# Putting 64-bit weights together as 32-bit values: the low words rounded to whole words in place, and the list of priorities replaced

## The chip, the cores and the metric

The kernel runs on one core of one Trainium2 chip. Its metric is the device time of one execution in microseconds. The core has TensorE (PE, matmuls into PSUM; PEld are its weight loads), VectorE (DVE), ScalarE (ACT), GpSimd (POOL) and SyncE (SP, which here issues every DMA). Each engine works through its own queue in order, and queues wait for one another through semaphores.

## The reference

A linear attention is followed by a two-layer block. There are 8 batches, 8 heads, 576 tokens and 64 columns a head. For q and k, `proj = x @ w_phi` has 128 features; the row's largest absolute value is taken off it, and the features are `exp(proj)` and `exp(-proj)` side by side. Then, per head,

```python
kv  = einsum('bhsf,bhsd->bhfd', k_p, v)
z   = sum over tokens of k_p
num = einsum('bhsf,bhfd->bhsd', q_p, kv)
den = einsum('bhsf,bhf->bhs', q_p, z)[..., None] + 1e-06
x   = num / den                      # 4608 tokens x 512
h   = x @ w_in                       # 512 -> 2048
out = relu(h) ** 2 @ w_out           # 2048 -> 512
```

The inputs of the attention are float32. `w_in` and `w_out` reach the kernel as 64-bit floating-point numbers.

## The kernel before, in words

**Attention.** Two heads form a pair, so there are 32 pairs (`NPAIR`), four to a batch. Keys and queries are projected on TensorE, DVE finds the largest absolute values and subtracts them (L602, L605, L714, L716), ACT takes the exponentials (L608, L610, L746, L748) and copies results out of PSUM (L310), and TensorE forms `kv`, `num` and `den`. The first six pairs (`early`, `EARLY = 6`) have a form of their own; the later ones go through `visit` and `late`, where POOL finds the largest absolute value over partitions (L943). The quotient of a pair is made at L808 and is scaled and split into two float16 parts for the block that follows (L827 or L834, then L830); both parts lie in a ring of tokens.

**The two-layer block.** The 4608 tokens are 18 chunks of 256. For each chunk, `moe` runs over eight slices `f` of 256 of the 2048 columns. The first matmuls (L1009) take the float16 parts of `w_in` (`win`), ACT and DVE form the square in two parts (L1018, L1020, L1022, L306), and the second matmuls (L1039) take `w_out` in three forms: a high part (`wh`), a low part and a bf16 copy (`wl`). The sums of one chunk over all `f` stand in two banks of PSUM, so one chunk's second matmuls are finished before the next chunk's begin. The first chunk therefore needs all sixteen pieces of weights.

**The weights.** `w_in` and `w_out` are cut into 8 pieces each, of 128 partitions x 1024 64-bit numbers, 1 MB a piece. `order_w` lists the sixteen pieces and `home_of` says which raw buffer each is loaded into. Buffers are used again: the load of a piece waits for the last reader of the piece before it there (`home_read`). The last six pieces share two buffers; pieces 3o, 6i, 7i and 7o follow one another in `x0` (the digit is `f`, i is `w_in`, o is `w_out`). A raw piece is a row of 2048 32-bit words: the low word of a number, then its high word. `join_words` makes a float32 of each pair of words:

- `size` (L450 on ACT, L452 on DVE) reads the high word as a float32 and scales it by 2 to the -111 into `u`. This brings the exponent into range.
- `low` (L456, ACT only) reads the low word as an unsigned number, scales it to between 0 and 7, and writes the rounded value, as one byte, over the lowest byte of the high word in the raw buffer. It comes after `size`, which reads that high word.
- `shift` (L460, DVE) moves `u` up by 3 bits.
- `join` (L463, DVE) takes the sign and the three low bits from the high word and joins them to `u`.

After the join, `most` (L480, ACT) writes absolute values of a piece of `w_in` over its low words, for a sum over the row. Every two such pieces give a power of two (L397 on TensorE, L403 to L408 on DVE), and `value_in` writes the two float16 parts (L529 or L530, then L532). A piece of `w_out` is split by `out_high` (L499 or L501) and `out_low` (L306 on POOL, L517 or L519). Four buffers `u` hold the joined words; `u` is taken by `size` and let go after the last of these splits. When all pieces are done, the room of `u` becomes the second half of the token ring.

**What sets the order.** Each operation is added to a `Plan` with an engine, a duration in microseconds, the operations it comes after, the buffers it uses and a rank. `other=` names a second engine with its own duration; the planner counts it as ready `LATER = 2.0` us later there. `lock=` is an allowance for the port that DVE and POOL share. `Plan.order` plays the durations through and, on each engine, takes the ready operation of the lowest rank. The instructions are issued in the resulting order, which is then fixed. The ranks of the operations whose given rank lies between -50 and 70 are replaced by those of a written-out list, `RANKS`, two characters a rank (`improve`). It holds 1107 of them, and covers the loads, the preparation of weights, the early pairs and the first part of what follows.

Of the kernel before, what the change touches and what calls it, by code (L numbers as in the profile page):

```python
# [292 lines left out]
def tile_kernel(ctx, tc, qp, kp, vp, w_phi, w_in, w_out, out):  # L293
    nc = tc.nc
    V, A, G, PE, SP = nc.vector, nc.scalar, nc.gpsimd, nc.tensor, nc.sync
    P = Plan()
# [129 lines left out]
    def fetch(n, f, of_in, rank):  # L426
        home = home_of[f, of_in]
        box = []
        src = w_in if of_in else w_out

        def load():
            box.append(cp.tile([128, 2048], I32, name=f"raw{f}{'io'[not of_in]}", tag=home))
            SP.dma_start(box[0], src[f])

        ld = P.add("SP", 0.47, load, [home_read[home]] if home in home_read else [], [], rank - 3.0 + 0.3 * n,
                   land=2.4, xfer=2.8)
        return ld, lambda: box[0][:, 0:2048:2], lambda: box[0][:, 1:2048:2], lambda: box[0].bitcast(U8)[:, 4:8192:8]

    def join_words(n, f, of_in, rank):

        home = home_of[f, of_in]
        key = [("u", n)]
        u = lambda: u_[0][n]
        ld, low_w, high_w, low_byte = fetch(n, f, of_in, rank)
        if of_in:
            spare[f] = low_w

        def size(E):
            if E is A:
                A.activation(out=u().bitcast(F32), in_=high_w().bitcast(F32), func=AF.Copy, scale=2.0 ** -111)  # L450
            else:
                V.tensor_scalar(out=u().bitcast(F32), in0=high_w().bitcast(F32), scalar1=2.0 ** -111, scalar2=None,  # L452
                                op0=ALU.mult)

        def low():
            A.activation(out=low_byte(), in_=low_w().bitcast(U32), func=AF.Copy,  # L456
                         scale=0.875 * 2.0 ** -29, bias=0.4995)

        def shift():
            V.tensor_scalar(out=u(), in0=u(), scalar1=3, scalar2=None, op0=ALU.logical_shift_left)  # L460

        def join():
            V.scalar_tensor_tensor(out=u(), in0=high_w(), scalar=word(0x80000007), in1=u(),  # L463
                                   op0=ALU.bitwise_and, op1=ALU.bitwise_or)
# [10 lines left out]
    def split_in(n, f, rank):  # L475
        o = join_words(n, f, True, rank)
        g, i = divmod(f, 2)

        def most():
            A.activation(out=spare[f]().bitcast(F32), in_=u_[0][n].bitcast(F32), func=AF.Abs, accum_out=wmax[g][:, i:i + 1])  # L480
# [652 lines left out]

DIGITS = "".join(chr(c) for c in range(33, 127) if chr(c) not in "\"\\'")[:90]
RANKS = (
    "B:HwDM8vA=A1EP2,D=EUc|UtLOUUS]TDUGLDQ8SJO=WTC3SmIyS[AhD=5!@-;CD.-THKHCQuCp?+^4IVH8MbT>X@[w[@c9[>FlEk"
    "`DCtgj^|BLM`D3`NMFGGAd@LLHR{ZDW<mq`Uv`XB`ma3QkZhJ4NaPVOCX@cuQ,Z5lBq;vUnT`wU;M>:UD/I^XIH[QAXLejY?dEOF"
    "ElP?W5NiXdS&CFBHB%A5/;,82rH70e557b4I7!-|%u-^-Z6A/x&:0$&>.f6];>3R2+;aC/2>IwE$ERUJH0F9B8P*RnVlbpFA.s2G"
    "1?1s0=;Q)J,/0J:hH#@T?i0b>a=Z:r1U4#4g4,3S0c-],k.42$11:?QWA@/V*?8J/a4;460p3*$<$;.F,a(()4#J&!$V({.1/W5U"
    "57:{Gi6Z4f>W>IBKPV<!9:G&ByAk]^GdDlA7Py[f[HLxIBFEEJA{<};^>_;gJ&2*0]&=*c.L-g<t71AqR(GfUyO<?9HwAM>wLo14"  # L1140
    ";/79=32@,&/r#=-},O+IAv.T3;#G8Y)A,2,X*x)2+%@(,K=&.d-K1%,^@@8}%94v5i:d<n<fE&Bl&k1k<&<h@k+W/12F1$85&#:Y"
    "=W@[8Z:;;F%H9V,7+8.1:s0.)xCO(Y.M+%+$.uAGDwL)>=FL>W?uEVERCp7nNb;pKw]+ZxSwS-QpcDVR[.FdQ.Q]SjXVI3G5ZoXC"
    "I,TzWzE,ZDS>JmG[BM@WE46AMPLVPAZ?JN=_GJ@5aYMU<OZ!PdXjQZI/9A9+D]Nd5?7bVr:<UkLF?!<pAL;jM=BoF8DO,+C9<[<d"
    "O{3|`+>$Zhd]]cRailV3QGW>_ZG5]BNHRROpBkKmFlUCHsY:M^]5SVDA:PA|7$1y;7Cg:TO[By7^3D*9?+CeK:SoS?J.LHScc)i*"
    "O[L@XsPIKiA.SX2UKhD%N}[%K_X*:wIGO3PC@oY[GkIk_U1k2w0D/5/O+q2Z1KCa=wC]@u=}Cs9}>4;69xE&?;=LR7MO>#H!TTUF"
    "T^VxeRM[VFTaP=XF6p?3Nv<6P#K9D4OTJjJbHPY.PkK;AmTDF-Tp[[MbN3<.MFFaX)0I8gJf?h:#H`FjJ;FZF;F;9aEME@A=HeOx"
    "Cd1[&8&g)-&6%N-20G,P-a7iFoGVRpYLY!D=P#W^A(P2Io?.Ou=JLNEFVEk9MjT*RsfzxjW/o2oPc)^2E;KkRbOjE=U<QN3Z;c:L"
    "A`YRI(UdT[HxZ!IVGE=WF=PCFm0gIw81BkGdSgHHRtEUAs>n]P_<ZRTCU#3ZFZMc]}K5GrR2FXZ2e`WBcPp_^5X7Y4MTL5N2UfF2"
    "T^FIGuO2IzQu:K;DIDA|K!Ch(l5K*`92MRCp:{IP@KKVPmUp<sOBKfN|PeI|6/KGAA0+B;PQR9=HG#GNN)V;WX>LLPK2Fa9|LqJx"
    "@CMsE:_WJFPYJUZFJX_0WyELDGN&Y^F4N]G.;#L0A_LNET4D=04PDo0)1ePn4u@tXp5lFdBEQiRuKIB,5[]%R$KhOdYr_.cE`)VK"  # L1150
    "ZYSkeUF_7vB^QG2gG;O|HUPPBi<F32B|DtIoQ>Z&_wXEd@W]MzZk[l]7a&FINNVXR#d-Oc^.I^XuQ`j9YnDGOiQ/UbF+JzAe@XN!"
    "YE4d;M?jH>DlQ<=R=KDB?}>mT>G7=AN.eBN$N$WdNm@DH{Mt>O@fY`OMGxR5UmH^R`2X7q<8?LOiM|6nBJAkGbM`J;LeHrD%_9H%"
    "PqF}V@k^ajgRxXjViI_^W_Xo_Pc?[eOoZeSvUyU/_me|d;c)J|Fm;P;hQ;Hr8vKyAXG(H0A_:37/MW9m9Y0}-7/.*!>O)>0k+,(u"
    "&M$G5%+u@G?1En+0>[K)N0?,:dNu<IRAMi=Y=V0qA&MqG;P9`nKUK(O#GdG>4&B}GtX{6JU*^?Z]NPN<NKB.GfJW8f[*T+V<]?G7"
    "40KrD$E$DD_^ZMR:NIO%MG]^cOYFMxPZSe_T].LB]R_yT^]3f?Y*Pm`EUDEpI&=I1o73)sAM8E;FO=IHAQAkFL9QKR2H-&.n)d=x"
    "AR2b?NNW9yC9N3XjeBhJ|<g&hdeP[Fc]]]P6c#U(J2AGJFCdByN/I}bKMRKcFJ=m?SJRDI@!MdRtXuQ7Ih>q`XILK@_,jVT|ITYL"
    "lNZsRH;I/qB=G<L0U*G`HlVoHp]2KZNP]}`S]IPgTMYHS+SFS/No?^I@Dr;*PG]hQ}e1TtMnTOWqZLgWYX`S^=W{[-^5G9XvT-[/"
    "D[U9Q@[wBl;qE5"
)


# [31 lines left out]
```

## Time and profile before

| | |
|---|---|
| time, median of 3 runs | 1078.0 us (1075.48 to 1078.98) |
| time of the profiled execution | 1078.0 us |
| its span, first to last instruction | 1076.2 us |
| instructions | 19519 |
| mean granted TensorE clock | 0.986 |
| L456, the rounding pass, ACT, 16 times | 2479 to 2606 ns each |
| L460, the shift, DVE, 16 times | 633 to 694 ns each |
| L463, the join, DVE, 16 times | 1210 to 1226 ns each |
| L450 / L452, the size pass | 12 on ACT, 4 on DVE |

A table of busy time by stage gives, for each stretch of the span in microseconds, the time that each engine was busy and how many instructions that was, then the granted clock of TensorE, the share of the DMA engines and the data rate. A row of the order of time gives the start and the duration in microseconds, the engine, the line of the program, what is written from what, the shapes, how many instructions the row merges, and in brackets how long the engine stood idle before it and for whom. Rows of one engine overlap a little at their ends, because a duration runs until the last write has landed.

### The profile page before, as it was taken

How to read it: one execution, taken by the hardware profiler on the slowest of the kernel's cores; microseconds unless marked ns; L12 is line 12 of the kernel's file. 1: busy time of each engine (PE TensorE's matmuls, PEld its weight loads, DVE VectorE, ACT ScalarE, POOL GpSimd, SP SyncE). 2: the span in 40 equal slices, each digit the busy share in tenths (PEclk: the TensorE clock that was granted, in tenths of full speed). 3: DMA queues.
4: the chain of work that ended last, by engine and by line, in shares of the span. 5: the costliest groups of instructions: out<-in, count | busy, mean ns of one | idle time of the engine just before them, and what ended most of it. 6: DMA issues, size and time to landing. Idle time of an engine off the chain costs nothing.

```text
span 1076.2 us, 19519 instructions
## 1 busy us (share of the span) xinstructions
PE 1038.8 (97%) x7762; PEld 711.0 (66%) x7762; DVE 730.6 (68%) x1546; ACT 655.2 (61%) x1133; POOL 137.0 (13%) x66
## 2 busy tenths in 40 slices
PE   6787899999999999999999999999999999999998
PEld 5554566666766666676666667666666666677775
DVE  5588788788877688888878777767786775111111
ACT  6799987756764557656666656665555665333333
POOL 0011113111120131101111111111011111000000
PEclk9897899999999999999999999999999999999999
DMA  9532350231122222121212111212110101000000
GB/s 362 210 115 89 114 169 32 56 104 56 48 56 65 66 65 67 56 76 56 73 48 76 50 60 44 65 56 75 39 58 28 48 10 42 12 21 20 1 21 20
DMA packets 66143, 73.47 MB, mean 68 GB/s; under 512 B 35204, under 2 KB 44036, under 8 KB 64004
## 3 DMA queue, kind: packets, MB, share of 16 engines
q1 hardware_dynamic: 66052, 72.22, 21.2%
q8 instruction: 61, 1.00, 0.4%
q14 instruction: 30, 0.25, 0.1%
HBM read 59.18 MB, written 12.99 MB: 67 GB/s over the span
## 4 chain that ended last, share of the span: by engine, by line
PE 88%; ACT 8%; DMA 2%; DVE 1%; issue 1%; SPq 0%; ACTq 0%
PE po L1039 35%; PE ph L1009 35%; PE pv L642 4%; PE pn L860 3%; PE pp L586 2%; PE pv L860 2%; PE pp L930 2%; PE pn L930 1%; PE pv L647 1%; ACT u L450 1%; PE pn L592 1%; DMA den<-sx 1%; DMA raw7i<-in_w_in_dram 1%; DMA v<-in_vp_dram 1%; ACT sx L549 0%
## 5 line engine op out<-in xcount | busy, mean ns | idle before, releaser
L1009 PE MATMUL ph<-ring,win 128*128 128x256 f16 x3456 | 402.7, 274 | 0.0
L1009 PEld LDWEIGHTS <-win 128*128 128x128 f16 x3456 | 338.0, 98 | 71.4 <-issue 8.5
L1018 ACT ACTIVATE r<-ph,cw 128x512 f32<-128x512 f32 x144 | 98.9, 687 | 235.4 <-PE ph L1009 234.9
L306 DVE TENSOR_TENSOR gl<-ph,gh 128x512 bf16<-128x512 f32 x144 | 98.5, 684 | 176.3 <-ACT ph L1022 172.5
L943 POOL PARTITION_ALL_REDUCE mx<-pt x52 | 115.9, 2229 | 616.5 <-ACT pt L310 453.6
L1039 PE MATMUL po<-wh,gh 128*128 128x512 f32 x576 | 171.5, 419 | 0.0
L1039 PE MATMUL po<-wl,gh 128*128 128x512 bf16 x576 | 149.6, 382 | 0.0
L1039 PE MATMUL po<-wl,gl 128*128 128x512 bf16 x576 | 148.0, 379 | 0.0
L1039 PEld LDWEIGHTS po<-wh,gh 128*128 128x128 f32 x576 | 98.4, 189 | 28.5 <-issue 9.1
L1039 PEld LDWEIGHTS <-gl 128*128 128x128 bf16 x576 | 56.3, 98 | 68.0
L1020 ACT ACTIVATE gh<-r 128x512 fp32r<-128x512 f32 x144 | 90.6, 629 | 4.4
L1039 PEld LDWEIGHTS <-gh 128*128 128x128 bf16 x576 | 44.8, 98 | 73.3 <-issue 39.7
L1022 ACT ACTIVATE ph<-r 128x512 f32<-128x512 f32 x144 | 84.1, 584 | 0.2
L642 PE MATMUL pv<-e,v 128*64 128x256 f32 x512 | 61.0, 380 | 0.0
L310 ACT ACTIVATE n<-pn 128x320 f32<-128x320 f32 (+1 forms) x32 | 13.8, 430 | 75.1 <-PE pn L860 74.6
L957 DVE SCALAR_TENSOR_TENSOR pt<-qe,zc,pt 128x576 f32<-128x576 f32 x52 | 42.2, 814 | 20.7 <-ACT pt L955 20.2
L306 DVE TENSOR_TENSOR qe<-pt,mx 128x576 f32<-128x576 f32 x52 | 39.1, 753 | 23.1 <-POOL mx L943 22.9
L948 ACT ACTIVATE qe<-qe 128x576 f32<-128x576 f32 x52 | 35.1, 674 | 27.9 <-DVE qe L306 27.9
L608 ACT ACTIVATE e<-e 128x512 f32<-128x512 f32 x64 | 39.7, 620 | 13.9 <-DVE e L605 13.7
L642 PEld LDWEIGHTS pv<-e,v 128*64 128x64 f32 x512 | 35.5, 137 | 15.4 <-issue 1.3
L955 ACT ACTIVATE pt<-qe,zc 128x576 f32<-128x576 f32 x52 | 40.2, 773 | 5.6 <-DVE zc L921 1.3
L894 DVE STREAM_TRANSPOSE kvs<-pv 128x256 f32<-128x256 f32 x26 | 11.6, 447 | 45.7 <-PE pv L860 44.1
(188 smaller groups left out, 1316.6 us busy)
## 6 DMA issues: line engine op xcount, KB each, us to landing
v<-in_vp_dram SPq DMA_DIRECT2D x32, 320.0 KB
k<-in_kp_dram SPq DMA_DIRECT2D x32, 288.0 KB
q<-in_qp_dram SPq DMA_DIRECT2D x32, 288.0 KB
rb<-rd SPq DMA_DIRECT2D x64, 144.0 KB
out_dram<-o SPq DMA_DIRECT2D x34, 256.0 KB
td<-kvs SPq DMA_DIRECT2D x26, 128.0 KB
kz<-td SPq DMA_DIRECT2D x104, 32.0 KB
raw0i<-in_w_in_dram SPq DMA_DIRECT2D x1, 1024.0 KB
```

The source lines that it names most:

```text
L306: eng.tensor_tensor(out=out_, in0=a, in1=b_, op=ALU.subtract)
L608: o = P.add("ACT", act_us(512), lambda n=n: A.activation(out=e_[n][:, :, 1, :], in_=e_[n][:, :, 0, :], func=AF.Exp, scale=-1.0), [o], [("e ...
L642: PE.matmul(out=to[64 * h:64 * h + 64, 0:256], lhsT=v_[p][:, t, h, :], rhs=e_[2 * p + h][:, t].rearrange("p s f -> p (s f)"), start=t == 0 ...
L860: PE.matmul(out=to[64 * h:64 * h + 64, :], lhsT=kz_[n][:, 128 * s_ + 64 * h:128 * s_ + 64 * h + 64], rhs=qe_[2 * n + h].rearrange("p (s x) ...
L943: o = P.add("POOL", par_us(S), lambda n=n, h=h: G.partition_all_reduce(mx_[n], pt_[p][:, h, :], channels=128, reduce_op=bass_isa.ReduceOp. ...
L955: o = P.add("ACT", act_us(S, 1), lambda h=h, qe=qe, y=y: A.activation(out=y(), in_=qe(0), func=AF.Copy, scale=zc_[p][:, 2 * h:2 * h + 1]), ...
L957: o = P.add("DVE", dve_us(S), lambda h=h, qe=qe, y=y: V.scalar_tensor_tensor(out=y(), in0=qe(1), scalar=zc_[p][:, 2 * h + 1:2 * h + 2], in ...
L1009: PE.matmul(out=ph[:, j, :], lhsT=win[w][:, t, 128 * ff:128 * ff + 128], rhs=ring[half][x][:, t, c0:c0 + T], start=k == 0, stop=k == 3 * K ...
L1018: o = P.add("ACT", act_us(512, 1), lambda: A.activation(out=r_[n], in_=ph_[bank], func=AF.Relu, scale=cw[:, f, 0:1]), [g1], [("ph", bank), ...
L1020: sq = P.add("ACT", act_us(512), lambda: A.activation(out=gh_[n], in_=r_[n], func=AF.Square), [o], [("r", n), ("gh", n)], Q)
L1022: o = P.add("ACT", 0.59, lambda: A.activation(out=ph_[bank], in_=r_[n], func=AF.Square), [o], [("ph", bank), ("r", n)], Q, other=("DVE", 0 ...
L1039: PE.matmul(out=po_[po[i][1]], lhsT=g[:, j, 128 * i:128 * i + 128], rhs=w[:, j, :], start=(ff == 0 and s == 0), stop=(ff == 2 * NFP - 1 an ...
```

## The change

The byte is no longer written. `low` writes its rounded value as a whole 32-bit word over the low word itself, so it waits only for the load, and it may run on ACT (planned at 1.15 us, as before) or on DVE (0.68). A pass of its own, `ends`, joins the sign of the high word to that low word, in place. The shift of `u` and the last join become one pass, which reads `u` and the low word. A piece still has four passes. All ranks in the list are replaced.

```diff
-        return ld, lambda: box[0][:, 0:2048:2], lambda: box[0][:, 1:2048:2], lambda: box[0].bitcast(U8)[:, 4:8192:8]
+        return ld, lambda: box[0][:, 0:2048:2], lambda: box[0][:, 1:2048:2]
...
-        def low():
-            A.activation(out=low_byte(), in_=low_w().bitcast(U32), func=AF.Copy,
-                         scale=0.875 * 2.0 ** -29, bias=0.4995)
-
-        def shift():
-            V.tensor_scalar(out=u(), in0=u(), scalar1=3, scalar2=None, op0=ALU.logical_shift_left)
+        def low(E):
+            to, of, a, b = low_w(), low_w().bitcast(U32), 0.875 * 2.0 ** -29, 0.4995
+            if E is A:
+                A.activation(out=to, in_=of, func=AF.Copy, scale=a, bias=b)
+            else:
+                E.tensor_scalar(out=to, in0=of, scalar1=a, scalar2=b, op0=ALU.mult, op1=ALU.add)
+
+        def ends():
+            V.scalar_tensor_tensor(out=low_w(), in0=high_w(), scalar=word(0x80000000), in1=low_w(),
+                                   op0=ALU.bitwise_and, op1=ALU.bitwise_or)
 
         def join():
-            V.scalar_tensor_tensor(out=u(), in0=high_w(), scalar=word(0x80000007), in1=u(),
-                                   op0=ALU.bitwise_and, op1=ALU.bitwise_or)
+            V.scalar_tensor_tensor(out=u(), in0=u(), scalar=3, in1=low_w(),
+                                   op0=ALU.logical_shift_left, op1=ALU.bitwise_or)
 
         sz = P.add("ACT", 1.15, lambda: size(A), [ld], key, rank, other=("DVE", 0.64, lambda: size(V), 4.0))
-        l = P.add("ACT", 1.15, low, [sz], [], rank)
-        o = P.add("DVE", 0.64, shift, [sz], key, rank, lock=4.0)
-        o = home_read[home] = P.add("DVE", 1.22, join, [o, l], key, rank, lock=4.0)
+        l = P.add("ACT", 1.15, lambda: low(A), [ld], [], rank, other=("DVE", 0.68, lambda: low(V), 4.0))
+        o = P.add("DVE", 1.22, ends, [l], [], rank, lock=4.0)
+        o = home_read[home] = P.add("DVE", 1.22, join, [sz, o], key, rank, lock=4.0)
         return o
...
 RANKS = (
-    "B:HwDM8vA=A1EP2,D=EUc|UtLOUUS]TDUGLDQ8SJO=WTC3SmIyS[AhD=5!@-;CD.-THKHCQuCp?+^4IVH8MbT>X@[w[@c9[>FlEk"
...
+    ">-88CNJ8R[-H?$EnS^A/FORAPUPUF1bR</BBDdK?[)T-Gvk=9djyUJ@&Ngk0WUW`QfRJc%^3[{itSEiwp/l$];JC[t>|K{-6H`,C"
...
```

More of the change, by code (lines that the diff above doesn't have):

```diff
@@ L19 @@
 U32 = mybir.dt.uint32
-U8 = mybir.dt.uint8
 AF = mybir.ActivationFunctionType
@@ L443, in join_words @@
         u = lambda: u_[0][n]
-        ld, low_w, high_w, low_byte = fetch(n, f, of_in, rank)
+        ld, low_w, high_w = fetch(n, f, of_in, rank)
         if of_in:
@@ L1135 @@
 RANKS = (
-    "B:HwDM8vA=A1EP2,D=EUc|UtLOUUS]TDUGLDQ8SJO=WTC3SmIyS[AhD=5!@-;CD.-THKHCQuCp?+^4IVH8MbT>X@[w[@c9[>FlEk"
[L1137 to L1155, printed above, removed]
@@ L1156 @@
-    "AR2b?NNW9yC9N3XjeBhJ|<g&hdeP[Fc]]]P6c#U(J2AGJFCdByN/I}bKMRKcFJ=m?SJRDI@!MdRtXuQ7Ih>q`XILK@_,jVT|ITYL"
-    "lNZsRH;I/qB=G<L0U*G`HlVoHp]2KZNP]}`S]IPgTMYHS+SFS/No?^I@Dr;*PG]hQ}e1TtMnTOWqZLgWYX`S^=W{[-^5G9XvT-[/"
-    "D[U9Q@[wBl;qE5"
+    ">-88CNJ8R[-H?$EnS^A/FORAPUPUF1bR</BBDdK?[)T-Gvk=9djyUJ@&Ngk0WUW`QfRJc%^3[{itSEiwp/l$];JC[t>|K{-6H`,C"
+    "M`J^CT]MX^?wC3[jU/J5Of9NYuFY:IOY6d)vMhT@O^FGU:d0D{S`9ySAV<rGLDJiKu5.<V;Wa*dsXtd)a$E(6wH7NT[g^:WPvDt2"
+    "lHsXs:xErHigT%Dbely3;2ejjox6rTo8]biYfvIlBvB^-XG*;L/)/|>48S77<]:H4K2:@s@aFALX@F>[IXTNRDItAd:r7e4P0c=J"
@@ new lines @@
+    ";XJi4bG$kei7M-H|6)a>BSLH2mBSEu:c7WGB?H@RO(*Z5m/+691I#Q6R.f%H5}>g3g&U#t.@Lb&l:`Gf9L/u4?(F/()|(o&k*m;P"
+    "0p+,;K4rOK*S.E0t6-4-$1(Y$A$w0q?$9W0^KH,-?}P?BM-{=O=q);AQ$=$D#f$E$0(<15(](9)b%,*&)Q%n,9$W+<#Q#-&7&y-%"
+    "#K3O<|&|,u1&1P80*x5gB@;h,t5L,_/v(K4}&#$R4E.x)k4A#w;P*C57#i11-A-T)tM9%HTcJ^:NKQ/IVhP_C,SFPN2q6>NFSe0r"
+    "I=<3,M5z;eK!)7($(m#=9j=(?Z2c(6;oBm:n/+6C-%8ZD29dDX@H^uW0;!,gA@QW@`B@.e4eF24{-8.y1v?wGu2E7e(e2AOL;+Vl"
+    ":UKq7bQ^@Z4^LY_U&9Fu,YgYAJ>&1qH|onK_XFL1ZoG>@-ehKZTc_T>leQ?)B1L[9{=DQu6dOCNE8<.UAe:sI2>*?+O@`fZSvvRL"
@@ new lines @@
+    "e3fwEUVZ6^Oh2T)N#J-X(x@llyNJS;N`dYB)DgdmK(R^G+Ai9.AUL-8m6w&VK$($1:<I&d,H5Y*..-D@A<ALSwCQ964bQZQ^J!G1"
+    "/T1LBX.?Cp=z58/V+,5BA/.xSSC=7)0qKrIFZk8L6,DPMwBEY[-p(c;3kcFpfhO|0WC{I`ehY}d3KG^n7Ge#QYUWL#cnV>IW5d=4"
+    "r{C[YP]Ia&ZOZII6Fw?q@C0.Jag8:a>^;-BOD!GRGTG%DMp+W@TMF(9,QPL1PTC+)J5X.8(m)`)[)*(=6v9mP3A?H9O9:/ECT>$H"
+    ",RN]?/)+/c%i)q+/Gx^(6i9A1RdbK5V<2g@ebtH$Aa<k5;UW^4iyk/lfi0j|u?udNgsMbeu0oqk{vAzxw[^E[<fIYh^Ue=U8T0LT"
+    ">p6JB(;h5^9{A*M/KMTaa<i>:VN%617L3+)6#D#D-UD-#DP,=?*-&X1+OKX|]cQhhAgkQBl]TOnuHft@Y:HqhGLu6A6C8uKvG$kP"
@@ new lines @@
+    "KHI[[/<G9N]XnjiY2[[LHS=KAras{CTlu?|_hSdygw|a|`ljiUo=WHP8j#YZHNbwfaJps1c+m{r,aQ^MiUJyHLPQ^?o)dSZ;R&RS"
+    "Op8}DbH9,/24,hPfNJe9?oRX5o5;CMQ9Q!Dr7[>(/{?y608+6`TiEce=|Wq=RhP)PT?aU{O/T*Q17fA-.D$3#729#99B?<ZjAF<M"
+    "H!=ZcpSXQ8?@]{Q3S;TNWq96;kCFHAG,^hXXl4]l^UZ9KrcgGcB;M9KhQ+K:TaZOpDbL_tGId@j)bso,o(kYa%dHuBr|dDW.W^b5"
+    "ww_qs+1Z:<WHMay]6g=o_x=.?nO-FcYmyD{/|,aQa#Uv|?|mcRL2FVgb4;534c2eW`@tU@/x5]5@)*<U6TPiCQ_.AHF&+K3JB7UV"
+    "P)T8/lX0<J9a;31;;694/H:j2)?:?BT!E|Lw<BRSI*H_W+@u4T5U<$:)BcN{F(;PE#Fw7kQ:MR[Hv&IzCS=#MkWRdug6V?yf{}tM"
@@ L1159 @@
+    "N4hprUuwbT]Ilpa>v5Nh;7IOJRo$npb:RholbCgoSrBURX:G.)I!=O/g;mS;)2%uZlM<auq;VTRfXPVi_YH0QieC?*F1T2B47%9G"
+    "Z/D}RPa?poIuCR>dQX2=.J3H4G&i)G/-(2/4(J2wF;3^8;9^KUU|DgE&3u3BF2=HAo.bcpbdB`M?ZACD[5.CHC`XKcaETPiVV.P&"
+    "C$HgMu?v=k[#e.K*H^_j[+e,Vl](OBae]Ug>[,UtiF^,|tx>s#TEn}bUI[pdgQj/f4PnN;::B<o!P}QFY`NjVNFWYZcwCwSFf]bx"
+    "h#B.S&BcI]OvWo8g@{Z1Zjf#rFxU](c#AIH*JW7??#4Hc?.Q9&)}XgL.[iNImeGY@U0)LMK:cf5^x(X[cOP[i_`mUi>D*sDOA*K#"
+    "WHbaOV`eTME>J."
 )
```

## The prediction

> **What bounds the kernel now.** I read the busy times and the slices of the page first, then a table of busy time by stage, then the order of time on each engine inside the stage that has the slack. All figures are of the one profiled execution, 1078.0 us long, of which the span is 1076.2 and 1.8 lie outside it; the median of the runs shown is 1078.0 too, so no correction stands between them.
>
> ```profile
> span 1076.2 us, 19519 instructions
> PE 1038.8 (97%) x7762; PEld 711.0 (66%) x7762; DVE 730.6 (68%) x1546; ACT 655.2 (61%) x1133; POOL 137.0 (13%) x66
> PE   6787899999999999999999999999999999999998
> DVE  5588788788877688888878777767786775111111
> ACT  6799987756764557656666656665555665333333
> ```
>
> ```profile
> core 0: us, PE busy (x) PEld busy (x) DVE busy (x) ACT busy (x) POOL busy (x), PEclk, DMA share, GB/s
> 0.00:40.00 40.00, 26.06 (x281) 19.02 (x281) 20.13 (x46) 26.16 (x46) 0.68 (x6) 1.00 0.94 365
> 40.00:170.00 130.00, 110.19 (x966) 73.42 (x967) 103.21 (x168) 120.36 (x170) 19.87 (x8) 0.88 0.34 109
> 170.00:1076.00 906.00, 902.50 (x6517) 618.56 (x6515) 607.27 (x1333) 508.64 (x920) 116.44 (x53) 1.00 0.17 49
> 118.70:170.00 51.30, 47.95 (x348) 32.55 (x347) 41.61 (x67) 46.43 (x62) 10.57 (x5) 0.94 0.36 122
> ```
>
> From 170 us on TensorE is busy 902.50 of 906.00 us: nothing there can be won or hidden, and whatever makes TensorE full earlier comes off the end one for one. Up to 40 us the DMA share is 0.94 and ACT is busy only 26.16 of 40: that stage waits for loads. Between 40 and 170 us TensorE idles 130 - 110.19 = 19.8 us, and its clock is 0.88 there, so up to 0.12 x 110.19 = 13.2 us more are lost to slow matmuls. In that stage ACT is the fullest engine, 120.36 of 130 us (0.926); DVE has 103.21 (0.79). After 118.70 TensorE idles only 51.30 - 47.95 = 3.4 us, so most of the slack, 16.4 us, lies between 40 and 118.70. That is where the sixteen weight pieces are put together beside the first six head pairs, and what TensorE waits for there is ACT:
>
> ```profile
> 96.13 2.15 PE L773 MATMUL pn<-qe,kz 128*32 128x288 f32 x16 [4.03 <-ACT n L310]
> 115.79 1.11 PE L737 MATMUL pp<-ident,pt 128*128 128x128 f32 x4 [3.84 <-ACT qe L748]
> ```
>
> **The change, part by part.** *The rounding pass on ACT (L456).* Today it reads 1024 unsigned 32-bit words, each 8 bytes from the last, and writes single bytes, also 8 bytes apart. An engine's rows overlap at their ends, so I price by the distance from start to start.
>
> ```profile
> 66.23 1.14 ACT L450 ACTIVATE u<-raw1o 128x1024 f32<-128x1024 f32 x1
> 67.28 0.47 ACT L310 ACTIVATE kvs<-pv 128x384 f32<-128x384 f32 x1
> ...
> 73.46 2.50 ACT L456 ACTIVATE raw1o<-raw1o 128x1024 uint8<-128x1024 uint32 x1
> 75.70 2.61 ACT L456 ACTIVATE raw3i<-raw3i 128x1024 uint8<-128x1024 uint32 x1
> ```
>
> The byte pass holds ACT for 75.70 - 73.46 = 2.24 us. A pass over the same 1024 words that reads 4 bytes at the same spacing and writes 4-byte values (L450) holds it for 67.28 - 66.23 = 1.05 us. The changed pass reads as the first and writes 4-byte words 8 bytes apart. L480 already writes 4-byte values into that place, in 39.97 - 38.97 = 1.00 us:
>
> ```profile
> 38.97 1.10 ACT L480 ACTIVATE raw1i<-u 128x1024 f32<-128x1024 f32 x1
> 39.97 0.18 ACT L480 ACTIVATION_READ_ACCUMULATOR raw1i<-u 128x1 f32 x1
> ```
>
> No row shows whole words from unsigned words on ACT. The bounds are 1.05 (L450, the price of reading and writing 4 bytes at all) and 2.24 (L456 as it is). I take 1.05: four of the five things that the new pass does (length, spacing of the read, spacing and width of the write) are in the 1.05 rows, and only the unsigned read is not. The gain is 1.19 us a pass.
>
> ```profile
> 0.00:40.00 40.00, 5.04 (x2) 1.00 0.94 365
> 40.00:118.70 78.70, 22.23 (x9) 0.85 0.33 101
> 118.70:170.00 51.30, 12.28 (x5) 0.94 0.36 122
> ```
>
> These are L456's passes by stage: 2 in the load-bound part, where 2 x 1.19 us buy nothing; 9 between 40 and 118.70; 5 after it. ACT in the stage falls by 14 x 1.19 = 16.7, from 120.4 to 103.7 us.
>
> By the Trainium skill ("ScalarE: Activation LUTs", section "What ACT_TABLE_LOAD costs"), ACT takes one element per cycle for every function, in fp32 and bf16 alike, and an ACTIVATE with immediate scale and bias 186 ns + 0.833 ns an element: an estimate of 1.04 us for these 1024. The 2.50 us row does not obey it. By that rule the types cannot be what makes the pass slow, the change of type would buy nothing, and the time would be that of the rival on the unsigned read, below.
>
> *The sign and the join on DVE.* The shift of u (L460) goes; its work is folded into the last join. A pass that takes the sign of the high word into the low word comes in; the join stays one pass.
>
> ```profile
> 29.48 1.23 DVE L463 SCALAR_TENSOR_TENSOR u<-raw1i,u 128x1024 int32<-128x1024 int32 x1 [1.12 <-ACT raw1i L456]
> 30.62 0.28 DVE L612 TENSOR_REDUCE kmt<-pn 128x1 f32<-128x128 f32 x1
> ...
> 72.90 0.68 DVE L452 TENSOR_SCALAR u<-raw3i 128x1024 f32<-128x1024 f32 x1
> 73.61 0.69 DVE L460 TENSOR_SCALAR u<-u 128x1024 int32<-128x1024 int32 x1
> 74.22 0.28 DVE L615 TENSOR_TENSOR et<-pn,kmt 128x128 f32<-128x128 f32 x1
> ```
>
> Old: 0.61 (L460) + 1.14 (L463). New: 1.14 + 1.14. DVE pays 0.53 us a piece more: 14 x 0.53 = 7.4 in the stage, 103.2 + 7.4 = 110.6 us. The new sign pass has both inputs and its output spaced; L463 has one input spaced. Bounds: 1.14, and twice that, 2.28, were the spacing to cost a full pass; I take 1.14 because the spaced L452 runs in 0.68 like the dense L460.
>
> *The second way, on DVE.* The rounding pass may now run on DVE, which the planner prices at 0.68. The nearest row is L452 (0.68, spaced read, same length), 0.61 from start to start; the upper bound is 1.14 (L463), were its types or its spaced write to halve the rate. Each pass so moved takes 1.05 off ACT and puts 0.61 on DVE. With DVE already the fuller engine by 110.6 to 103.7, I take none moved on balance for the sum. Fully levelled, the two would have (110.6 + 103.7) / 2 = 107.2 us each.
>
> *The order inside a piece.* The byte pass had to wait for the size pass, since it overwrote a byte of the word that the size pass reads. The new pass needs the load alone. Before, the path of a piece was 1.05 + 2.24 + 1.14 = 4.4 us; now it is 1.05 + 1.14 + 1.14 = 3.3, with the size pass beside it. Behind the sign pass on DVE wait that engine's maxima and subtractions for the next head pair, which is in the 7.4 us. The last pieces share one raw buffer, so each load waits for the piece before it:
>
> ```profile
> 116.34 0.33 SPq L433 DMA_DIRECT2D raw6i<-in_w_in_dram  x1
> ...
> 136.37 0.33 SPq L433 DMA_DIRECT2D raw7i<-in_w_in_dram  x1
> ...
> 151.82 0.33 SPq L433 DMA_DIRECT2D raw7o<-in_w_out_dram  x1
> ```
>
> If only that chain counted, its three pieces give 3 x 1.1 = 3.3 us.
>
> *The list.* All 1107 ranks are replaced, so the order on every queue, SP's loads among them, changes in the stages up to 170 us. The old list was made with 1.15 us for a pass that takes 2.24; the new one prices the same pass at 1.15. For the order itself the trace bounds it by its largest stall that is due to order alone:
>
> ```profile
> 38.24 0.74 ACT L549 ACTIVATE sx<-v 128x640 bf16<-128x640 f32 x1 [5.49 <-DMA den<-sx]
> ```
>
> ACT stands 5.49 us in front of a late load. The new order may lose this (a gain of 5.5) or have one more (a loss of 5.5); I take zero.
>
> *The sum.* Way one, by the fullest engine: DVE with 110.6 us, as full as ACT is today (0.926), needs 110.6 / 0.926 = 119.4 us for what takes 130: 10.6 us less. Way two, by place: the 9 passes before 118.70 us give 9 x 1.19 = 10.7; the five after it lie beside a TensorE that has 3.4 us of idle time left, and I count nothing for them (without that cover they would be worth 5 x 1.19 = 6.0 more). Both say 10.6. Forecast: 1078.0 - 10.6 = 1067.4 us. Its own range runs from the chain alone (1078.0 - 3.3 = 1074.7) to the whole ACT relief (1078.0 - 16.7 = 1061.3).
>
> **The rivals.**
> *The unsigned read is what costs 2.24 us.* For it: no 1.05 us row reads unsigned words. Against it: the byte write is just as new to those rows. Then ACT keeps 120.4 us unless passes move. All 14 on DVE make it 110.6 + 14 x 0.61 = 119.1 us, and 119.1 / 0.926 = 128.6: 1.4 us won; none moved wins nothing. About 1077.
>
> *The raw-buffer chain sets the end.* For it: the three issues above, 15 to 20 us apart. Against it: TensorE idles only 3.4 us after 118.70. 1074.7.
>
> *The new order also loses the 5.49 us stall*, beside the full 16.7: 1078.0 - 22.2 = 1055.8. For it: 33 us of idle time and slow clock are there to be won. Against it: up to 40 us the DMA share is 0.94, and an order cannot make loads faster.
>
> *Slower: DVE becomes the bound, through the port that it shares with POOL.*
>
> ```profile
> 79.78 2.62 POOL L306 TENSOR_TENSOR wl<-u,wh 128x1024 bf16<-128x1024 f32 x1 [13.13 <-ACT wh L499]
> 120.63 2.74 POOL L306 TENSOR_TENSOR wl<-u,wh 128x1024 bf16<-128x1024 f32 x1 [1.50 <-DVE wh L501]
> ```
>
> ```profile
> 80.08 2.93 DVE L808 TENSOR_TENSOR rb<-n,rb 128x576 f32<-128x576 f32 x1
> ...
> 121.18 3.27 DVE L532 SCALAR_TENSOR_TENSOR win<-u,cw,win 128x1024 f16<-128x1024 f32 x1
> ...
> 125.56 1.28 DVE L532 SCALAR_TENSOR_TENSOR win<-u,cw,win 128x1024 f16<-128x1024 f32 x1
> ```
>
> A DVE pass that starts inside one of POOL's runs till POOL has ended: 3.27 for 1.28 us, 2.0 lost. POOL is busy 19.87 of the 130 us, 0.15. Were the planner to send all 14 rounding passes to DVE, 28 passes are new there (sign and rounding): 28 x 0.15 x 2.0 = 8.4 us on top of 119.1 make 127.5, and 127.5 / 0.926 = 137.7: 7.7 later, 1085.7. It decides once DVE carries more than the 120.4 us that ACT has now, that is, from 120.4 - 110.6 = 9.8 us of moved passes and held ports on. Against it: the planner counts 2 us against a pass on its second engine, and the removed shift was open to the same hold. By the Trainium skill ("SBUF — State Buffer", section "Who interferes with whom") a DVE instruction with two SBUF inputs, or in a two-port mode, and a POOL one that reads SBUF exclude each other for the whole instruction; the four rows agree with it.
>
> **How the numbers follow.** About 0.3%, 3.2 us, is what a measurement can tell from no change. Chances: forecast 0.55 (faster 0.93, same 0.05, slower 0.02 of it), unsigned read 0.16 (0.3, 0.5, 0.2, for the order may fall either way), buffer chain 0.09 (0.65, 0.3, 0.05), stall lost as well 0.08 (all faster), DVE bound 0.12 (0, 0.3, 0.7). Faster: 0.512 + 0.048 + 0.058 + 0.080 = 0.70. Same: 0.028 + 0.080 + 0.027 + 0.036 = 0.17. Slower: 0.011 + 0.032 + 0.004 + 0.084 = 0.13. The range reaches from 1055, just past the case where the stall is lost as well (1055.8), to 1080, past the unsigned read (1077) and into the DVE case by as much as the 3.2 us of a measurement; what it leaves out is most of the DVE case, some 0.09, and about 0.06 below.
>
> **What would show it.** The rounding pass, written as int32 from uint32, at about 1.14 us on ACT and 0.68 on DVE: right; at 2.5: the unsigned read. The sign pass at 1.2 us on DVE. Between 40 and 170 us ACT busy well under 120 and DVE over it or near; a TensorE that is full, with no idle time of 3 us or more, from about 108 instead of 118.70; the last of the weight pieces joined near 155 instead of 165. DVE over 0.93 of that stage beside idle time of TensorE that ends on DVE would show the slower case. The forecast is wrong if ACT's relief is there and TensorE's idle time before its full stage is still 16 us or more.

## The result, and the profile after

The changed kernel takes 1064.59 us (median of 4 runs, 1063.47 to 1066.1) against 1077.55 us before: a ratio of 0.9889, 95% interval 0.9876 to 0.9903. That is faster by 12.0 us (10.4 to 13.4), where 10.6 were forecast. Below, each ratio is turned into microseconds by (ratio - 1) x 1077, since the runs of the kernel before that stand beside an experiment differ by a microsecond or two from one experiment to the next.

The page of the changed kernel, its span, its busy times and three rows of the 40 slices:

```profile
span 1064.3 us, 19450 instructions
PE 1028.1 (97%) x7676; PEld 705.8 (66%) x7762; DVE 745.1 (70%) x1549; ACT 632.0 (59%) x1130; POOL 136.2 (13%) x66
PE   7788999999999999999999999999999999999998
DVE  6799987987977868889878777867686775111111
ACT  6798876656666556756666655665565565333333
```

TensorE is at 9 tenths or more from the fifth slice on, before only from the sixth (a slice is 27 us). Of its matmuls 86 have no record here (7676 against 7762 weight loads), so its busy time after 170 us isn't compared. Busy time by stage of the changed kernel (engines in the order PE, PEld, DVE, ACT, POOL, then clock, DMA share, GB/s):

```profile
0.00:40.00 40.00, 29.22 (x320) 21.42 (x320) 31.05 (x59) 28.00 (x50) 0.68 (x6) 1.00 0.95 366
40.00:170.00 130.00, 113.65 (x1008) 74.56 (x1012) 115.17 (x190) 104.43 (x177) 24.27 (x9) 0.96 0.33 109
```

Between 40 and 170 us ACT is down from 120.36 to 104.43 us, DVE up from 103.21 to 115.17. TensorE's idle time there fell only from 19.8 to 16.4 us; its clock rose from 0.88 to 0.96, so by the estimate of the prediction slow matmuls cost up to (1 - 0.96) x 113.65 = 4.5 us where they cost up to 13.2. In the load-bound 40 us before it DVE does 31.05 us of work where it did 20.13.

The passes of a piece in the changed kernel, by line: the rounding pass on ACT (L457) and on DVE (L459), the sign pass (L462).

```profile
L457 ACT ACTIVATE raw3o<-raw3o x1: 1263/1263/1263, 28.9 to 28.9; 128x1024 int32<-128x1024 uint32 x1
L457 ACT ACTIVATE raw5i<-raw5i x1: 1107/1107/1107, 34.5 to 34.5; 128x1024 int32<-128x1024 uint32 x1
...
L459 DVE TENSOR_SCALAR raw6o<-raw6o x1: 676/676/676, 138.9 to 138.9; 128x1024 int32<-128x1024 uint32 x1
...
L462 DVE SCALAR_TENSOR_TENSOR raw7o<-raw7o x1: 1234/1234/1234, 150.2 to 150.2; 128x1024 int32<-128x1024 int32 x1
```

The first two are the longest and the shortest of twelve on ACT; four are on DVE. From start to start the next work on ACT follows after 1.01 to 1.11 us, so the passes are at the prices taken. The order of time on SP, and then on ACT for piece 3i:

```profile
125.48 0.33 SPq L432 DMA_DIRECT2D raw7i<-in_w_in_dram  x1
...
139.34 0.35 SPq L432 DMA_DIRECT2D raw7o<-in_w_out_dram  x1
```

```profile
13.43 1.12 ACT L457 ACTIVATE raw3i<-raw3i 128x1024 int32<-128x1024 uint32 x1 [0.48 <-DMA raw3i<-in_w_in_dram]
...
76.93 1.17 ACT L449 ACTIVATE u<-raw3i 128x1024 f32<-128x1024 f32 x1
```

The last pieces' loads are issued 10.9 and 12.5 us earlier than before (136.37 and 151.82), about as much as the whole gain. That the loads are what sets the end is not shown by it. And piece 3i is rounded at 13.43 us, 63 us ahead of its size pass (L449): the old order could not do that, for the byte pass waited for the size pass, which needs one of four `u` buffers.

### The profile page after: what moved, and what is told of

The parts are those of the page before. It is cut to its first block, busy times and chain, and to the rows that moved or that the text cites. A ratio compares the mean times of both kernels' runs of the same rounds, so it can differ in the third digit from the quotient of the medians.

```text
span 1064.3 us, 19450 instructions
## 1 busy us (share of the span) xinstructions
PE 1028.1 (97%) x7676; PEld 705.8 (66%) x7762; DVE 745.1 (70%) x1549; ACT 632.0 (59%) x1130; POOL 136.2 (13%) x66
## 4 chain that ended last, share of the span: by engine, by line
PE 86%; DVE 6%; DMA 4%; ACT 3%; issue 1%; SPq 0%; DVEq 0%; ACTq 0%
PE po L1042 34%; PE ph L1012 33%; PE pv L645 5%; PE pn L863 3%; PE pp L589 2%; PE pv L863 2%; PE pp L933 2%; DMA den<-sx 1%; PE pn L933 1%; PE pv L650 1%; PE pn L595 1%; DVE u L466 1%; DMA rd<-rc 1%; DVE rb L811 1%; DMA rb<-rd 1%
## 5 line engine op out<-in xcount | busy, mean ns | idle before, releaser
L946 POOL PARTITION_ALL_REDUCE mx<-pt x52 | 113.4, 2180 | 619.1 <-ACT pt L309 437.7
L1042 PE MATMUL po<-wl,gh 128*128 128x512 bf16 x504 | 134.1, 381 | 4.9
L645 PE MATMUL pv<-e,v 128*64 128x256 f32 x512 | 63.4, 388 | 7.3 <-ACT kz L309 5.4
L964 DVE STREAM_TRANSPOSE yt<-pt 128x576 f32<-128x576 f32 x52 | 40.4, 776 | 1.5
```

What stands on the lines that cost most here:

```text
L645: PE.matmul(out=to[64 * h:64 * h + 64, 0:256], lhsT=v_[p][:, t, h, :], rhs=e_[2 * p + h][:, t].rearrange("p s f -> p (s f)"), start=t == 0 ...
L946: o = P.add("POOL", par_us(S), lambda n=n, h=h: G.partition_all_reduce(mx_[n], pt_[p][:, h, :], channels=128, reduce_op=bass_isa.ReduceOp. ...
L964: o = P.add("DVE", dve_us(S), lambda n=n, y=y: V.transpose(yt_["y", n - 2 * EARLY], y()), [o], [("pt", p), ("yt", ("y", n - 2 * EARLY))], ...
L1042: PE.matmul(out=po_[po[i][1]], lhsT=g[:, j, 128 * i:128 * i + 128], rhs=w[:, j, :], start=(ff == 0 and s == 0), stop=(ff == 2 * NFP - 1 an ...
```

## The experiments

**The price of the byte pass alone.** The old order, with one word changed in it:

```diff
-            A.activation(out=low_byte(), in_=low_w().bitcast(U32), func=AF.Copy,
+            A.activation(out=low_w(), in_=low_w().bitcast(U32), func=AF.Copy,
```

> The kernel before, its list and its order of instructions, with one edit: the rounding pass on ACT writes a whole 32-bit word over the low word instead of a byte into the high word. The join is as it was, so the three lowest bits of every weight keep the high word's own three lowest bits: the low word is left out of the weights. No sign pass, no new list, DVE's work unchanged. Theory (the price of the byte pass is the gain): ACT is relieved by 14 x 1.19 = 16.7 us between 40 and 170 us, and the time falls by 10 to 17 us, to 1061 to 1068. Rival (the new list, or the freer order inside a piece, is the gain): less than 4 us, 1074 or more.

Measured: 1059.88 us, ratio 0.9843 (0.9826 to 0.9859), 16.9 us faster. By stage, in that run:

```profile
40.00:170.00 130.00, 118.44 (x1059) 81.02 (x1065) 115.33 (x202) 113.77 (x189) 25.23 (x10) 0.94 0.37 114
```

The price of the pass is worth more than the whole gain of the change, and nearly all of the 16 x 1.19 = 19.0 us that ACT is spared comes off the end. The theory stands; what comes with the change besides must cost about 5 us.

The edit also does a second thing. The byte lay in the high word, which the join reads; the whole word does not, so the join no longer reads what the rounding pass writes. In the trace before, DVE waits 11.6 us for that pass in front of twelve joins (who waited for L456):

```profile
  DVE u L463: 11.6, 12
```

In this run's trace there is no such wait. Every join there starts 0.06 us or more after the rounding pass of its piece has ended, so with the shorter pass the wait would have cost next to nothing even if the join still had to have it. How much of the 16.9 us is ACT's time and how much these waits of DVE, no run separates.

**No rounding at all.** The old order again, without the pass:

```diff
-            A.activation(out=low_byte(), in_=low_w().bitcast(U32), func=AF.Copy,
-                         scale=0.875 * 2.0 ** -29, bias=0.4995)
+            pass
...
-            V.scalar_tensor_tensor(out=u(), in0=high_w(), scalar=word(0x80000007), in1=u(),
+            V.scalar_tensor_tensor(out=u(), in0=high_w(), scalar=word(0x80000000), in1=u(),
```

> The kernel before, its list and its order, without any rounding pass: the low word is left out, and the join takes the sign alone, so the three lowest bits of each weight are zero. ACT has 16 passes fewer than before. It prices ACT in the old order once more, past the point where the byte pass became a word pass (1059.9 with 16 passes of 1.05 us left). Theory (every microsecond that ACT is spared in the preparation of the weights comes off the end at 0.6 to 1.0, as the runs so far have it: 16.6 for 19.0 in the old order, 0.65 per us in the new): 16.8 us less on ACT, 10 to 17 us less time, 1043 to 1050. Rival (with the byte price gone the loads, DVE or TensorE's own work hold the end): 1055 or more.

Measured: 1061.05 us, ratio 0.9861 (0.9845 to 0.9878), 15.0 us faster. Here the theory fell: another 16.8 us taken off ACT bought nothing. In the old order the rounding pass holds the end down to a word pass of 1.05 us and no further. That fits with the waits of DVE, which were gone already with the whole words, but is not shown by a run of its own. The last load (7o) is issued at 134.86 us here and at 137.10 with the whole words, and the time is no shorter, so an earlier last load is not always a gain.

**The new passes in the old order.** Whole words, no shift, and at the join's place the sign pass and the new join:

```diff
-            V.tensor_scalar(out=u(), in0=u(), scalar1=3, scalar2=None, op0=ALU.logical_shift_left)
+            pass
...
-            V.scalar_tensor_tensor(out=u(), in0=high_w(), scalar=word(0x80000007), in1=u(),
-                                   op0=ALU.bitwise_and, op1=ALU.bitwise_or)
+            V.scalar_tensor_tensor(out=low_w(), in0=high_w(), scalar=word(0x80000000), in1=low_w(),
+                                   op0=ALU.bitwise_and, op1=ALU.bitwise_or)
+            V.scalar_tensor_tensor(out=u(), in0=u(), scalar=3, in1=low_w(),
+                                   op0=ALU.logical_shift_left, op1=ALU.bitwise_or)
```

> The kernel before, its list and its order, with the changed kernel's arithmetic put into it, whole and exact: the rounding pass writes whole words on ACT (all 16 pieces), the shift is not issued, and at the join's place DVE does the sign pass and the joining pass one behind the other. Against the run with whole words in the old order (1059.9) DVE has 16 x 0.53 = 8.5 us more, 7.4 of them after 40 us. Theory (the sign pass costs what lies on DVE's path, the new list brings nothing of its own): 3 to 7 us more than that run, 1063 to 1067, level with the changed kernel's 1064.6. Rival (the new list pays for part of the sign pass): 1068 or more. Second rival (the sign pass is free, and the new list is the worse one): 1060 to 1062, faster than the changed kernel.

Measured: 1072.16 us, ratio 0.9967 (0.9953 to 0.9981), 3.6 us faster than before. Against the whole words alone that is 13.3 us slower, for 8.5 us of work on DVE. Not all of it is that work: the sign pass reads the rounded word, so DVE waits for the rounding pass again (2.1 us in three waits in this trace). The first rival has it: the sign pass is dear in the old order, and the new order wins 12.0 - 3.6 = 8.4 us back.

**What the new order wins with.** The changed kernel, its list and its engines, but each rounding pass issued only behind the size pass (on ACT) or in front of the join (on DVE), and each sign pass in front of the join:

```diff
+        done = {}
+
         def size(E):
+            done["size"] = True
+            size_of(E)
+            if done.get("low") is A:
+                low_of(A)
+
+        def low(E):
+            done["low"] = E
+            if E is A and "size" in done:
+                low_of(A)
+
+        def ends():
+            pass
+
+        def join():
+            if done["low"] is V:
+                low_of(V)
+            ends_of()
+            join_of()
+
...
```

> The changed kernel with its list and its operations on the same engines, whole and exact, but the early places are not used: a rounding pass on ACT is issued only when the size pass of its piece has been, and a rounding pass on DVE and every sign pass only right in front of the joining pass. In the profile of the changed kernel 6 of 12 rounding passes on ACT, 2 of 4 on DVE and 7 of 16 sign passes lie before 40 us, with the joins of their pieces up to 65 us later, so some 6 us of ACT's work and some 9 us of DVE's move into the stage after 40 us. Theory (what the new order wins over the old one, 7.6 us, is the work put where engines have room, which the rounding in place allows since it holds no joined-word buffer): 5 to 12 us more than the changed kernel, 1070 to 1077. Rival (the 7.6 us are the rest of the list, other work in a better order): 0 to 3 us more.

Measured: 1076.12 us, ratio 1.0005 (0.9995 to 1.0014): the time of the kernel before.

```profile
0.00:40.00 40.00, 31.28 (x320) 23.06 (x320) 24.98 (x52) 23.57 (x46) 0.68 (x6) 0.96 0.94 365
40.00:170.00 130.00, 107.14 (x959) 68.93 (x960) 115.54 (x177) 103.74 (x172) 22.19 (x8) 0.95 0.34 109
```

The first 40 us lose 6.1 us of DVE's work and 4.4 of ACT's against the changed kernel, and from 40 to 170 us TensorE is busy 6.5 us less. With no early places the new list wins nothing at all. The theory stands, with one limit: the order was not planned anew for the late passes. The run shows what this list loses without its early places, not what a list made without them could reach; the old order with the same passes took 1072.16.

**How much room ACT has in the new order.** A second pass on ACT copies each rounded word onto itself:

```diff
                 A.activation(out=to, in_=of, func=AF.Copy, scale=a, bias=b)
+                A.activation(out=to, in_=to, func=AF.Copy)
```

> The changed kernel in its own order, with a second pass on ACT that copies each rounded word onto itself behind the rounding pass: 12 pieces pay 1.05 us more on ACT, 6 of them after 40 us, which is about the old price of the byte pass. Theory (DVE has become the fullest engine, 115.2 of 130 us against ACT's 104.4, so ACT has room): the 6.3 us leave ACT at 110.7, still under DVE, and the time rises by 0 to 3 us. Rival (ACT still sets the pace): 6 to 13 us more.

Measured: 1071.83 us, ratio 0.9963 (0.9950 to 0.9976): 8.0 us slower than the changed kernel for 12.6 us on ACT. The theory of the fullest engine fell: ACT, at 104.43 us against DVE's 115.17, has no such room. The second pass is also in the way of DVE, for the sign pass has to wait for it: DVE's waits for these passes on ACT before its sign passes come to 10.5 us in this trace, 4.4 in the changed kernel's. So the 8.0 us are the price of a longer pass in that place, not of ACT's busy time alone. The same second pass behind the six early rounding passes alone (with `not in` for the six late ones):

```diff
+                if (f, of_in) in ((3, True), (0, True), (4, True), (3, False), (1, False), (5, True)):
+                    A.activation(out=to, in_=to, func=AF.Copy)
```

> The changed kernel in its own order, the second pass on ACT (1.05 us, each rounded word copied onto itself) only behind the six rounding passes that ACT does before 40 us (pieces 3i, 0i, 4i, 3o, 1o, 5i): 6.3 us more on ACT there. Theory (the new order puts these passes where ACT waits for loads, and there they cost nothing): 0 to 1.5 us more than the changed kernel, 1064 to 1066. Rival (a pass costs the same wherever it stands, so half of the 7.2 us that all twelve cost): 3 to 4 us more.

> The same with the second pass only behind the six rounding passes that ACT does after 40 us (pieces 0o, 2o, 4o, 5o, 7i, 7o). Theory (there ACT still sets the pace, as the run with all twelve has it): 5.5 to 7.5 us more than the changed kernel, 1070 to 1072. Rival: 3 to 4 us more.

Measured: 1068.71 us (0.9931, 0.9912 to 0.9949) for the early six and 1068.5 us (0.9929, 0.9912 to 0.9945) for the late six, 4.5 and 4.3 us slower than the changed kernel, with some 2.5 us of uncertainty each. For the early six the theory (0 to 1.5 us) is out and the rival stands. For the late six the two can't be told apart: some 1.8 to 6.8 us hold the rival's 3 to 4 and a part of the theory's 5.5 to 7.5. The measured middle is 4.4 us for 6.3 us on ACT in either place, and both together, 8.8, agree with the 8.0 for all twelve. So a place before 40 us is not free.

**DVE's side.** Without the sign pass:

```diff
         def ends():
-            V.scalar_tensor_tensor(out=low_w(), in0=high_w(), scalar=word(0x80000000), in1=low_w(),
-                                   op0=ALU.bitwise_and, op1=ALU.bitwise_or)
+            pass
```

> The changed kernel in its own order without the sign pass: the sign of every weight is left out. DVE loses 16 passes of 1.14 us, 9 of them after 40 us, 10.3 us there. Theory (DVE is the bound of that stage now): 115.2 falls to 104.9 us, level with ACT, and the time falls by 5 to 10 us below the changed kernel, to 1055 to 1060. Rival (loads and the chain through the raw buffers set the pace): less than 2 us.

Measured: 1061.45 us, ratio 0.9865 (0.9849 to 0.9880), 2.6 us faster than the changed kernel, with some 2.2 us of uncertainty, for 18.2 us taken off DVE. The theory is out, and the rival's size (less than 2 us) fits: in the new order the sign passes cost little. That loads and raw buffers are the reason, as the rival has it, is not shown. And DVE's passes that POOL holds: in the order of time of the changed kernel's DVE, seven between 40 and 170 us last 1.6 to 2.2 us beyond their usual time, of which three are

```profile
56.18 2.81 DVE L833 SCALAR_TENSOR_TENSOR ring<-rb,cb,ring 128x576 f16<-128x576 f32 x1
...
100.46 2.73 DVE L522 CAST wl<-u 128x1024 bf16<-128x1024 f32 x1
...
156.22 2.93 DVE L811 TENSOR_TENSOR rb<-n,rb 128x576 f32<-128x576 f32 x1
```

The run that gives POOL's part to DVE:

```diff
-        last = [P.add("POOL", 2.4, lambda: lower(G), at, key, rank, lock=0.0, other=("DVE", 1.23, lambda: lower(V), 4.0)),
+        last = [P.add("POOL", 2.4, lambda: lower(V), at, key, rank, lock=0.0, other=("DVE", 1.23, lambda: lower(V), 4.0)),
```

> The changed kernel in its own order, whole and exact, but the eight low parts of w_out that POOL makes (2.4 us each, with a DVE pass held beside seven of them for 1.6 to 2.2 us more than its own time, 13.7 us in all) are made by DVE at the same place in the order, 1.14 us each, 9.1 in all. Theory (the port that DVE shares with POOL costs DVE more than the work itself would): DVE is spared some 4.6 us between 40 and 170 us, and the time falls by 0.5 to 3 us below the changed kernel. Rival (the held passes stand where DVE has time, the new 1.14 us where it has none): 0 to 4 us more.

```profile
40.00:170.00 130.00, 113.84 (x1020) 74.86 (x1021) 111.88 (x202) 104.20 (x178) 4.77 (x2) 0.96 0.35 114
```

Measured: 1064.77 us, ratio 0.9891 (0.9874 to 0.9909), no different from the changed kernel's 0.9889. DVE is spared 3.3 us, the held passes are gone, and the time does not move: the difference is 0.2 us, with some 2.4 us of uncertainty, so the upper end of both sides is out and neither is shown.

**The old list under the new operations.** Only the list is put back:

```diff
 RANKS = (
-    ">-88CNJ8R[-H?$EnS^A/FORAPUPUF1bR</BBDdK?[)T-Gvk=9djyUJ@&Ngk0WUW`QfRJc%^3[{itSEiwp/l$];JC[t>|K{-6H`,C"
...
+    "B:HwDM8vA=A1EP2,D=EUc|UtLOUUS]TDUGLDQ8SJO=WTC3SmIyS[AhD=5!@-;CD.-THKHCQuCp?+^4IVH8MbT>X@[w[@c9[>FlEk"
...
```

> The changed kernel with the old list of ranks; nothing is left out. The same ranks now stand for other operations (the third and fourth of each piece) and other durations. Theory (a list belongs to the operations it was searched for): far slower than both kernels, 1130 to 1200, by the planner's own sum 1169.7. Rival (a list is a loose set of priorities, and the order within a piece matters little): within 10 us of the changed kernel.

Measured once: 1154.65 us. The theory stands: a list means something only with the operations and durations that it was made for.

**Which types make a pass slow.** Behind the last work of the changed kernel, three passes of each kind on ACT and then on DVE, each writing the same place:

```diff
...
+        words = pa[:, 0:2048:2].bitcast(U32)
+        probe(pb[:, 0:2048:2], words)
+        probe(pb.bitcast(U8)[:, 0:8192:8], words)
+        probe(pb.bitcast(U16)[:, 0:4096:4], words)
+        probe(pb.bitcast(BF16)[:, 0:4096:4], words.bitcast(F32))
+        probe(pb.bitcast(BF16)[:, 0:2048:2], words.bitcast(F32))
+        probe(pb.bitcast(U8)[:, 0:1024], words)
+        probe(pb.bitcast(U8)[:, 0:8192:8], words.bitcast(F32))
```

> The changed kernel, with rounding passes of 1024 values behind its last work, alone on ACT and then alone on DVE, three of each: whole words 8 bytes apart, bytes 8 bytes apart, 16-bit integers 8 bytes apart, bf16 8 bytes apart, bf16 4 bytes apart, dense bytes (all from unsigned or float words 8 bytes apart), and bytes 8 bytes apart from float words. Theory (narrow spaced writes are what costs): every spaced write under 4 bytes takes about 2.5 us on ACT, whatever it reads, and whole words and dense bytes about 1.1. Rival (only the turning into an 8-bit integer costs): bytes 2.5 dense and spaced, the 16-bit forms 1.1. On DVE, which no row shows: 0.7 for whole words, 0.7 to 1.4 for the others.

The order of time of that run, three passes to a row (start, then time of all three):

```profile
1063.18 3.36 ACT L1143 ACTIVATE win<-win 128x1024 int32<-128x1024 uint32 x3 [3.80 <-DVE win L1138]
1066.58 2.15 DVE L1145 TENSOR_SCALAR win<-win 128x1024 int32<-128x1024 uint32 x3 [3.43 <-ACT win L1143]
1068.76 7.46 ACT L1143 ACTIVATE win<-win 128x1024 uint8<-128x1024 uint32 x3 [2.22 <-DVE win L1145]
1076.25 3.97 DVE L1145 TENSOR_SCALAR win<-win 128x1024 uint8<-128x1024 uint32 x3 [7.53 <-ACT win L1143]
1080.26 7.46 ACT L1143 ACTIVATE win<-win 128x1024 uint16<-128x1024 uint32 x3 [4.04 <-DVE win L1145]
...
1091.75 7.46 ACT L1143 ACTIVATE win<-win 128x1024 bf16<-128x1024 f32 x3 [4.04 <-DVE win L1145]
...
1103.24 4.09 ACT L1143 ACTIVATE win<-win 128x1024 bf16<-128x1024 f32 x3 [4.03 <-DVE win L1145]
1107.37 2.30 DVE L1145 TENSOR_SCALAR win<-win 128x1024 bf16<-128x1024 f32 x3 [4.16 <-ACT win L1143]
1109.69 3.37 ACT L1143 ACTIVATE win<-win 128x1024 uint8<-128x1024 uint32 x3 [2.36 <-DVE win L1145]
...
1115.28 7.46 ACT L1143 ACTIVATE win<-win 128x1024 uint8<-128x1024 f32 x3 [2.21 <-DVE win L1145]
```

Per pass, ACT takes 7.46 / 3 = 2.49 us for every narrow write 8 bytes apart, from unsigned or float words, to bytes, 16-bit integers or bf16; 1.12 for whole words 8 bytes apart and for dense bytes. The rows follow the order of the calls, so the first bf16 row is 8 bytes apart and the second, 4.09 / 3 = 1.36, is 4 apart. DVE has the same steps: 0.72 for whole words, 1.32 for bytes 8 bytes apart, 0.77 for bf16 4 apart. The theory stands: it is the narrow, spaced write.

## Why the prediction was right

The time (1067.4 against 1064.59) and the sign were right. The prices of the single passes were right for the reasons given; that the sum came so near is in good part luck. Step by step:

- **The rounding pass** was priced at 1.05 us from the rows of L450 and L480; in place it lasts 1.11 to 1.26 us as a row, like L450. The choice of the lower bound was right, and the unsigned read is free. ACT's fall in the stage, 16.7 us forecast, is 120.36 - 104.43 = 15.9, but made up otherwise: of 14 rounding passes six are left there on ACT, and other work has moved in.
- **The sign pass** was priced at 1.14 us from L463; its rows are those of L463. That spacing costs nothing for whole words was right too.
- **Way two of the sum was wrong.** It counted nothing for two passes before 40 us and five after 118.70, and so 10.7 us. Whole words alone give 16.9 us (15.2 to 18.7), so the five count too; whether the two do, that run does not say. In the new order 6.3 us more on ACT cost about 4.4, before 40 us as well as after. A TensorE that idles only 3.4 us in a stretch was not cover: its clock there was 0.94 besides, up to 0.06 x 47.95 = 2.9 us more, and with the whole words it is busy 50.96 of these 51.30 us at a clock of 1.00.
- **Way one of the sum came near for a wrong reason.** It let the fullest engine alone set the stage. 12.6 us on ACT, the less full one, cost 8.0 us, and 18.2 us off DVE, the fuller one, gave 2.6. An order fixed beforehand ties both engines together, and the busy share does not say which of them is waited for. DVE's waits for the rounding pass go with the time in three runs (11.6 us before, 4.4 in the changed kernel, 10.5 with the second pass), but not in the old order with the new passes (2.1 us, and 1072.16 us of time). The prediction priced that wait only inside one piece's path.
- **The term left out** is the order inside a piece. I priced it as a chain (3.3 us) and the list as zero. What counted is that the rounding and the sign pass hold no `u` buffer any more, so fifteen of the 32 stand before 40 us. With them put back late under the same list, the whole gain is gone.
- **The sum as it is:** -16.9 for whole words, +13.3 for the sign pass where it would have stood in the old order, -8.4 for the new order with its early places; together -12.0. Way two had -10.7 for the first, and nothing for the sign pass and the list. Its misses, -6.2, +13.3 and -8.4 us, come to -1.3: that is the luck.
- **Slow matmuls** were named (up to 13.2 us) and priced at nothing. By the same estimate they fell by up to 8.7 us between 40 and 170 us, more than the idle time there did (3.4). After a wait of 4.03 us at 96.13 us, 16 matmuls of L773 took 2.15 us in the trace before, and 1.18 behind a wait of only 1.11 us:

```profile
74.65 1.18 PE L773 MATMUL pn<-qe,kz 128*32 128x288 f32 x16 [1.11 <-DVE et L615]
```

  In the changed kernel only one wait between 40 and 170 us is longer than 2 us, where there were four, and the clock in the stage's last 51 us is 1.00 where it was 0.94:

```profile
118.70:170.00 51.30, 47.10 (x345) 31.87 (x344) 45.94 (x81) 36.01 (x60) 10.14 (x4) 1.00 0.27 91
```

  The row behind the wait of 4.03 us agrees with the Trainium skill ("TensorE: Matmul & The Clock Gate", section "Part 1: The HAM clock gate (the "warmup" mystery)"), by which the array falls to half its clock after an idle window of about 3.4 us. A shorter wait did it too: in the changed kernel TensorE waits 1.82 us, until 79.84 us, and the clock from 80 to 83 us is 0.50. There the measurement decides. A removed wait of this kind is worth its own length and the slow work behind it, 2.15 - 1.18 = 0.97 us in the row at 96.13 alone.

- **The rivals.** The unsigned read is excluded by the types run. The buffer chain alone, 3.3 us, was too little, though the loads on it moved by as much as the end. The stall of 5.49 us was not lost: ACT still stands 4.18 us, until 40.99 us, in front of a pass of the same kind. The slower case did not come: DVE has 115.17 us, under the 120.4 from which it was to decide. Its mechanism is there, seven held passes with 13.7 us in all where the trace before has five with 9.4 us (L808, L404, L532, L629 and L633, 1.6 to 2.2 each), but taking it away changed nothing that could be measured.
- **The signs that were named.** TensorE has no wait of 3 us or more after 43.83 us (108 was forecast), the last piece is joined at 152.8 us (155), and DVE has 115.17 of 130 us, 0.89, under the 0.93 of the slower case. The sign of failure, 16 us or more of idle time before the full stage, is not there: between 40 and 118.70 us TensorE idles 78.70 - 66.56 = 12.1 us, where it was 16.4. Of the gain only a part thus shows as less idle time there; by these figures the rest lies in the clock and in the first 40 us, where TensorE is busy 29.22 us instead of 26.06.

What stays open is why 6.3 us on ACT cost about as much before 40 us, where the DMA share is 0.95, as after it, and how the gain divides between ACT's time and DVE's waits for it. No run with all of the arithmetic beat the changed kernel; whole words in the old order (0.9843) is faster, but leaves the low word out.

## What to carry to other kernels

Before an engine is called slow, its rows are to be compared with another pass of the same length on the same engine: here 2.5 us stood beside 1.1 for one and the same count of elements, and the cause was the type and spacing of the write. When operations are put on engines in an order that is fixed beforehand, a pass that starts from its load alone, and writes in place, can be worth more than its duration says, since it can be put where others wait. A stretch in which TensorE is nearly full did not hide the preparation of what it needs next.

## What the runs showed of the hardware

- A write of 1024 values of 1 or 2 bytes, each 8 bytes from the last, takes ACT 2.49 us against 1.12 for 4-byte values with the same spacing or for dense bytes, and DVE 1.32 against 0.72. What is read (unsigned or float) makes no difference. At 4 bytes apart, bf16 costs 1.36 on ACT and 0.77 on DVE.
- The Trainium skill ("ScalarE: Activation LUTs", section "What ACT_TABLE_LOAD costs") has one rate for every ACTIVATE in fp32 and bf16; by its formula an estimate of 1.04 us for these 1024. The whole-word row, 1.12 us a pass, comes near it; the bf16 row 8 bytes apart, 2.49, does not, and the measurement decides.
- Seven DVE passes that started while POOL made its part of `w_out` lost 1.6 to 2.2 us each, 13.7 us in all, and the time did not change by more than its uncertainty of 2.4 us when they were freed.
